# Routed attention with a GELU feed-forward block on one Trainium2 core: where and when the 64-bit weights are rounded

## The chip, the cores and the metric

The kernel runs on one NeuronCore of a Trainium2 chip. The engines named below are TensorE (PE in the profile, with its weight loads as PEld), VectorE (DVE), ScalarE (ACT), GpSimd (POOL) and SyncE (SP, which here only issues DMAs). The metric is the device time of one execution in microseconds (us). The kernel before was timed five times: median 1053.18 us, from 1050.35 to 1054.77 us.

## What is computed

Attention with 4 batches, 8 heads, 768 tokens and head size 64. Every query and every key is assigned to the nearest of 16 centroids of its head, and a query sees only the keys of its own cluster:

```python
q_assign = argmax(q_n @ c_n); k_assign = argmax(k_n @ c_n)      # per head
mask = q_assign[:, :, :, None] == k_assign[:, :, None, :]
scores = where(mask, scale * q @ k.T, -1e9)
x = softmax(scores) @ v            # -> (3072, 512)
h = x @ w_in                       # 512 -> 2048
g = h * 1 / (1 + exp(-1.702 * h))
out = g @ w_out                    # 2048 -> 512
```

q, k, v and the centroids are fp32. The two weight matrices come as 64-bit floats, and the kernel makes fp32 numbers of them on the chip: this is the "rounding" that the change is about.

## The kernel before, in words

**Units and turns.** A pair is two heads of one batch; there are 16 pairs. The scores of a pair are made transposed, in units of 128 keys by 384 queries of both heads; 12 units make a pair, 192 units the whole. Six units that share their queries are a group g (32 groups). The main loop runs over turns t = 0 to 97, with two units each in turns 0 to 95. In a turn TensorE makes the scores (L393) and, in the first batch (turns 0 to 23), adds a one-hot product (L407) that pushes masked scores away; ScalarE takes the exponentials (L418); in the later batches VectorE masks them (L429); GpSimd adds the units of a group up (L439); TensorE multiplies the units of the turn before with v (L450). Two turns after the end of a group `normalise(g)` sums over the keys on TensorE (L462), VectorE takes the reciprocal (L465) and multiplies (L467). `check(g)` lets ScalarE add up the reciprocals and a function of them (L477, L479): these sums decide at the end whether the fast path was safe.

**Preparation.** `prep_*` steps of the next pairs (transposes L271, products with the centroids L285, the assignment L296 to L317, the one-hots L358 or the spread codes L332) are dealt to turns by the table `prep_at`.

**The feed-forward block inside the turns.** When group 3 is normalised (turn 13) the first half of batch 0 goes into the queue `half_ffn`: 16 pieces `first` (L516, four matmuls with `w_in`, then `gelu`) and 12 pieces `second3` (L496, four matmuls with `w_out`). When group 7 is normalised, 48 pieces of the other half follow in `ffn` (L545 and L496). A turn adds a rate to the counter `owed` and takes as many pieces: 28/11.5 = 2.43 a turn from `half_ffn`, 0.62 a turn from `ffn`, the latter until 8 pieces are left. These 8 run after the last turn, before the remaining three batches go through a feed-forward stage of their own (`first7` with L733, `second7` with L790).

**Rounding a weight chunk.** The weights are cut into NW = 32 chunks of 128 x 512 numbers, 16 of `w_in` and then 16 of `w_out`. SyncE loads a chunk as pairs of 32-bit words into one of three `raw` buffers (L155). `split_w` takes the exponent bits (L168) and the mantissa bits (L170) of the high words on VectorE, and turns each into its floating-point part on ScalarE (L172, L174). One call later `join_w` puts the sign to the power (L180), adds the low words (L183) and multiplies (L186), all on VectorE. `round_next()` issues the load of chunk i+2, `split_w(i)` and `join_w(i-1)`. It is called once in turns 1, 2, 4, 5, 6, 8, 9 and 10, and from turn 12 on twice a turn, three times in odd turns, until all is done; `round_to` calls it where a piece needs a chunk that is not there.

**What sets the order.** The program is under a manual schedule: each engine runs its instructions in the order in which the code writes them. So what stands in front of what on an engine is read directly from the loop. Tile pools bound how far engines may drift apart: three PSUM banks `m` (`bank()`) for preparation, normalising and feed-forward pieces, two PSUM score buffers, four `A` buffers, three `raw`, two `e`.

Of the kernel before, what the change touches and what calls it, by code (L numbers as in the profile page):

```python
# [38 lines left out]
def fast(  # L39
# [26 lines left out]
    nc = tc.nc  # L66
# [20 lines left out]
    const = ctx.enter_context(tc.tile_pool(name="const", bufs=1))  # L87
# [15 lines left out]
        name="dram", bufs=2, space=bass.MemoryType.DRAM))  # L103
# [3 lines left out]
    def bank():  # L107
        return ps_m.tile([P, 512], FP32, name="m")
# [17 lines left out]
    def load_v(p):  # L126
# [16 lines left out]
    w_chunks = [  # L143
        (w[:, c, n:n + WN],
         src.bitcast(I32)[c * P:(c + 1) * P, 2 * n:2 * (n + WN)])
        for w, src, n_c, n_n in ((w_in, moe_w_in, NCH, DF),
                                 (w_out, moe_w_out, NF, DM))
        for n in range(0, n_n, WN) for c in range(n_c)]
    NW = len(w_chunks)
    w_raw, w_pow = {}, {}  # L150

    def load_w(i):
        if i < NW:
            t = wp.tile([P, WN, 2], I32, name="raw")
            nc.sync.dma_start(out=t.rearrange("p n t -> p (n t)"),  # L155
                              in_=w_chunks[i][1])
            w_raw[i] = t

    EXP = 0x7FF00000

    def split_w(i):

        hi = w_raw[i][:, :, 1]
        w = w_chunks[i][0]
        e = wp.tile([P, WN], I32, name="e", bufs=2)
        nc.vector.tensor_scalar(out=e, in0=hi, scalar1=EXP, scalar2=None,  # L168
                                op0=ALU.bitwise_and)
        nc.vector.tensor_scalar(out=w.bitcast(I32), in0=hi, scalar1=0xFFFFF,  # L170
                                scalar2=None, op0=ALU.bitwise_and)
        nc.scalar.activation(out=e, in_=e, func=AF.Relu, scale=8.0,  # L172
                             bias=low[:, 0:1])
        nc.scalar.activation(out=w, in_=w.bitcast(I32), func=AF.Copy,  # L174
                             scale=2.0 ** -20, bias=1.0)
        w_pow[i] = e

    def join_w(i):
        raw, e, w = w_raw.pop(i), w_pow.pop(i), w_chunks[i][0]
        nc.vector.scalar_tensor_tensor(  # L180
            out=e, in0=raw[:, :, 1], scalar=-2 ** 31, in1=e,
            op0=ALU.bitwise_and, op1=ALU.bitwise_or)
        nc.vector.scalar_tensor_tensor(  # L183
            out=w, in0=raw.bitcast(U32)[:, :, 0], scalar=2.0 ** -52, in1=w,
            op0=ALU.mult, op1=ALU.add)
        nc.vector.tensor_tensor(out=w, in0=w, in1=e.bitcast(FP32),  # L186
                                op=ALU.mult)

    w_done = [0]

    def round_next():
        i = w_done[0]
        if i < NW:
            load_w(i + 2)
            split_w(i)
        if 0 < i <= NW:
            join_w(i - 1)
        w_done[0] += 1

    def round_to(n):  # L200
        while w_done[0] <= min(n, NW):
            round_next()

    load_qk(1, 0)
# [6 lines left out]
    nc.vector.tensor_copy(out=ident_h, in_=ident)  # L211
    half = const.tile([P, 1], FP32, name="half")
    nc.vector.memset(half, 0.5)
    low = const.tile([P, 1], FP32, name="low")
    nc.vector.memset(low, -896.0 * 2.0 ** 23)
    top = const.tile([P, 1], FP32, name="top")
    nc.vector.memset(top, 2.0 * LIMIT)
    twos = const.tile([P, D], FP32, name="twos")
# [7 lines left out]

    hot = hp1.tile([P, NJ * 4, 32], BF16, name="hot")
    nc.vector.memset(hot, 0.0)
    row_sums = const.tile([P, 2, 2 * NPAIR], FP32, name="sums")

# [9 lines left out]
                            op0=ALU.add)  # L240
# [230 lines left out]
    recs = {}  # L471

    def check(g):


        rec = recs.pop(g)
        nc.scalar.activation(out=rec, in_=rec, func=AF.Copy,  # L477
                             accum_out=row_sums[:, 0, g:g + 1])
        nc.scalar.activation(out=rec, in_=rec, func=AF.Relu, bias=top[:, 0:1],  # L479
                             scale=-2.0 * LIMIT * LIMIT,  # L480
                             accum_out=row_sums[:, 1, g:g + 1])
# [22 lines left out]
    half_ffn, ffn = deque(), deque()  # L504
# [63 lines left out]
    NT = NU // 2  # L568
    TG = NJ // 2
    TB = 2 * HP * TG  # L570

    prep_at = {}
    for p in range(1, NPAIR):
        b, hp = divmod(p, HP)
        for i in range(2 if p == 1 else 0, len(PREP)):
            if p == 1:
                t = (i - 2) // 2
            elif b == 0:
                t = (hp - 2) * TG + 1 + i // 2
            else:  # L580
                t = b * TB + TG * hp - (7, 7, 6, 6, 4, 3, 2)[i]
# [5 lines left out]
    def prep(p, i):  # L587
        if i == 0 and p:
            load_v(p)
        PREP[i](p)  # L590
        if i in (1, 3) and loads:
            load_qk(*loads.popleft())

    rate = (NF + NH * (NF // 4)) / (TB / 2 - 0.5)
    owed = 0.0
    for p, i in [(0, i) for i in range(6)] + [(1, i) for i in range(2)]:
        prep(p, i)
# [2 lines left out]
    for t in range(NT + 2):  # L600
        us = range(2 * t, 2 * t + 2) if t < NT else ()
        for u in us:
            scores(u)
        if t == 0:
            prep(0, 6)
        for u in us:
            part(u)
        for u in us:
            exps(u)
        second_half = t >= TB // 2  # L610
        if second_half:
            round_next()
        if recs:
            check(*recs)
        for u in us:
            mask(u)
        work = sorted(prep_at.get(t, ()), key=lambda w: PREP[w[1]] != prep_near)
        while work and PREP[work[0][1]] == prep_near:
            prep(*work.pop(0))
        if 1 <= t <= NT:  # L620
            for u in range(2 * t - 2, 2 * t):
                values(u)

        todo = half_ffn or (ffn if len(ffn) > NF // 2 else ())
        owed += (rate if half_ffn else 0.62) if todo else -owed
        g = (t - 2) // TG if t >= 2 and (t - 2) % TG == TG - 1 else None
        if g is not None and second_half:
            normalise(g)
        for p, i in work:
            prep(p, i)  # L630
        if g is not None and not second_half:
            normalise(g)
        if recs and t < TB:
            check(*recs)
        if second_half or t and t % 4 != 3:
            round_next()
        while owed >= 1 and todo:
            todo.popleft()()
            owed -= 1
        if second_half and t % 2:  # L640
            round_next()
    check(*recs)
    qcode.clear()
    att.close()
# [181 lines left out]
    for b in range(1, B):  # L826
        for f in range(FB):
            if b == 1:
                sums_z(f)
            first7(b, f, *XT)  # L830
            sums_w((b - 1) * FB + f + 2)
        for n in range(NH):
            sg = sums_g(n)
            if (b, n) == (B - 1, 1):
                ps = bank()
                nc.tensor.transpose(out=ps[0:1, 0:P], in_=ok1, identity=ident)
                nc.vector.tensor_reduce(out=okt, in_=ps[0:1, 0:P], axis=AX.X,
                                        op=ALU.min)
                nc.vector.tensor_scalar(out=bad, in0=okt, scalar1=-1.0,
                                        scalar2=1.0, op0=ALU.mult, op1=ALU.add)  # L840
            if (b, n) == (B - 1, NH - 1):
                is_bad = nc.values_load(bad[0:1, 0:1], min_val=0, max_val=1)
            second7(b, n, sg)
            if n == 1 and b < B - 1:
                XT = sums_x(b + 1)
            if (b, n) == (B - 1, 0):


                ok = const.tile([P, 2, 2 * NPAIR], FP32, name="ok")
                nc.vector.tensor_scalar(out=ok, in0=row_sums, scalar1=LIMIT,  # L850
                                        scalar2=None, op0=ALU.is_le)
                ok1 = const.tile([P, 1], FP32, name="ok1")
                nc.vector.tensor_reduce(out=ok1, in_=ok, axis=AX.XY, op=ALU.min)
# [439 lines left out]
```

## Time and profile before

| what | value |
|---|---|
| median of 5 runs | 1053.18 us |
| the profiled execution, its own time | 1052.68 us |
| its span in the trace | 1050.9 us |
| mean granted TensorE clock | 0.982 |
| PE busy in the span | 998.9 us (95%) |
| DVE busy | 686.3 us (65%) |
| ACT busy | 365.3 us (35%) |
| POOL busy | 389.1 us (37%) |

The span is 1.8 us shorter than the execution's time; that lies around it and is no part of the trace. The profile's page has the busy shares in 40 slices of the span, the chain of work that ended last, and groups of instructions with their count, busy time and mean duration. The trace answers the same for any stretch (a window), for one source line, and as a timeline of single instructions. A line such as "L439 POOL TENSOR_TENSOR sum<-sum,A" says: line 439 of the kernel, on GpSimd, writes tile `sum` from `sum` and `A`.

The turns can be told in the timeline by their scores (L393). Turn 1 starts at 17.2 us of the span, turn 5 at 40.6, turn 9 at 65.1, turn 14 at 89.6, turn 17 at 136.9, turn 20 at 167.5, turn 21 at 187.8, turn 26 at 249.1, turn 32 at 280.1. The last scores (turn 95) start at 584.7, the 8 pieces after the turns at 594.8, and the feed-forward stage at 609.9.

### The profile page before, as it was taken

Reading aid. Unit: us, or ns where it says so; the run is one execution under the profiler, and the core shown is the slowest. Engines: PE = TensorE matmul, PEld = TensorE weight load, DVE = VectorE, ACT = ScalarE, POOL = GpSimd, SP = SyncE. Lnnn points to the kernel's source line nnn. Section 1 sums busy time; section 2 is a strip of 40 time slices with the busy share of each in tenths; the row PEclk is TensorE's granted clock in tenths of the full one; section 3 lists DMA queues with packets and bytes.
Section 4 is the critical chain, followed back from the end, with each engine's and each line's share of the span. In section 5 each row is a group of like instructions: output and inputs, shape, how many; then the busy total and the mean of one; then the engine's idle time right before and its main releaser. Section 6 shows DMA issues by size and latency. Waiting matters only on the chain.

```text
span 1050.9 us, 12464 instructions
## 1 busy us (share of the span) xinstructions
PE 998.9 (95%) x4574; PEld 584.1 (56%) x4574; DVE 686.3 (65%) x1079; ACT 365.3 (35%) x697; POOL 389.1 (37%) x280
## 2 busy tenths in 40 slices
PE   7887798999999999999999899999999999999997
PEld 3333353445544455443544355688755788655886
DVE  3889998415877788776877667743477634576431
ACT  3655465323555555445555322200022200122000
POOL 2554322223666466655567847600022100120000
PEclk9998899999999999999999999999999999999999
DMA  7523354122002320032100000000000000000000
GB/s 198 144 66 106 126 152 138 38 65 63 17 0 61 83 71 8 17 75 61 26 1 1 1 11 0 1 21 21 21 0 1 1 21 21 21 0 1 21 21 23
DMA packets 66117, 45.24 MB, mean 43 GB/s; under 512 B 52096, under 2 KB 60032, under 8 KB 66048
## 3 DMA queue, kind: packets, MB, share of 16 engines
q1 hardware_dynamic: 65904, 44.33, 14.9%
q8 instruction: 38, 0.62, 0.3%
q14 instruction: 31, 0.25, 0.1%
q10 hardware_dynamic: 144, 0.03, 0.0%
HBM read 38.04 MB, written 6.31 MB: 42 GB/s over the span
## 4 chain that ended last, share of the span: by engine, by line
PE 83%; DVE 11%; ACT 2%; issue 1%; POOL 1%; DMA 1%; DVEq 0%; ACTq 0%; POOLq 0%
PE b L790 21%; PE b L733 21%; PE s L393 11%; PE o L450 9%; PE m L496 8%; PE m L545 4%; DVE short L465 2%; PE m L516 2%; PE m L271 2%; DVE A L429 2%; PE m L462 2%; DVE e L168 1%; PE m L285 1%; DVE e L180 1%; DVE w_in L186 1%
## 5 line engine op out<-in xcount | busy, mean ns | idle before, releaser
L439 POOL TENSOR_TENSOR sum<-sum,A 128x768 f32<-128x768 f32 x128 | 235.7, 1841 | 201.4 <-DVE A L429 104.6
L429 DVE SCALAR_TENSOR_TENSOR A<-qb,code,s 128x384 f32<-128x384 uint8 x288 | 157.6, 608 | 94.8 <-ACT s L418 82.1
L393 PE MATMUL s<-T,T 64*128 64x384 f32 x768 | 158.6, 525 | 13.2 <-ACT A L418 9.0
L450 PE MATMUL o<-A,inv 128*64 128x384 f32 x768 | 147.0, 502 | 1.1 <-DVE A L429 1.1
L418 ACT ACTIVATE s<-s 128x768 f32<-128x768 f32 x144 | 109.4, 793 | 83.4 <-PE s L393 72.6
L724 DVE TENSOR_TENSOR G<-b,G 128x384 f32<-128x384 f32 x168 | 93.4, 556 | 51.8 <-PE b L733 45.0
L671 POOL TENSOR_TENSOR W<-w_in 128x256 f32<-128x256 f32 x24 | 17.7, 738 | 263.8 <-PE b L733 262.8
L393 PEld LDWEIGHTS s<-T,T 64*128 64x128 f32 x768 | 66.2, 189 | 86.4 <-issue 23.9
L724 DVE TENSOR_TENSOR y<-b,y 128x256 f32<-128x256 f32 x54 | 22.1, 423 | 130.1 <-PE b L790 93.8
L486 ACT ACTIVATE th<-G 128x384 f32<-128x384 f32 x96 | 50.2, 523 | 159.0 <-DVE G L724 98.4
L733 PE MATMUL b<-x,w_in 128*128 128x384 f32 x288 | 101.2, 486 | 0.0
L450 PEld LDWEIGHTS o<-A,inv 128*64 128x64 f32 x768 | 47.2, 137 | 86.5 <-issue 81.3
L439 POOL TENSOR_TENSOR sum<-A 128x768 f32<-128x768 f32 x32 | 59.5, 1861 | 93.0 <-ACT A L418 43.3
L465 DVE RECIPROCAL short<-m 128x384 f32<-128x384 f32 x32 | 81.7, 2552 | 13.7 <-PE m L462 13.6
L487 DVE SCALAR_TENSOR_TENSOR G<-th,G 128x384 f32<-128x384 f32 x96 | 68.6, 714 | 16.9 <-ACT th L486 14.2
L733 PEld LDWEIGHTS b<-x,w_in 128*128 128x128 f32 x288 | 54.7, 190 | 37.9 <-issue 0.5
L733 PE MATMUL b<-x,W 128*128 128x384 f32 x192 | 69.8, 486 | 0.0
L516 PE MATMUL m<-x,w_in 128*128 128x384 f32 x128 | 51.3, 559 | 15.6 <-ACT short L291 4.9
L790 PE MATMUL b<-Z,G 128*128 128x256 f32 x288 | 65.1, 379 | 0.0
L790 PE MATMUL b<-w_out,G 128*128 128x256 f32 x288 | 63.6, 379 | 0.0
L790 PEld LDWEIGHTS b<-w_out,G 128*128 128x128 f32 x288 | 54.6, 190 | 8.1
L790 PEld LDWEIGHTS b<-Z,G 128*128 128x128 f32 x288 | 54.7, 190 | 7.4
(115 smaller groups left out, 1310.6 us busy)
## 6 DMA issues: line engine op xcount, KB each, us to landing
raw<-in_moe_w_in_dram SPq DMA_DIRECT2D x16, 512.0 KB, 3.9
raw<-in_moe_w_out_dram SPq DMA_DIRECT2D x16, 512.0 KB, 3.7
in<-in_q_dram SPq DMA_DIRECT2D x32, 192.0 KB, 3.0
in<-in_k_dram SPq DMA_DIRECT2D x32, 192.0 KB, 4.0
inv<-in_v_dram SPq DMA_DIRECT2D x16, 384.0 KB, 4.3
out_dram<-y SPq DMA_DIRECT2D x15, 256.0 KB, 2.1
qb<-line SPq DMA_DIRECT2D x12, 192.0 KB, 3.3
out_dram<-y SPq DMA_DIRECT2D x18, 128.0 KB, 1.8
```

What stands on the lines that cost most here:

```text
L393: nc.tensor.matmul(out=ps[:, a, 0:HALF], lhsT=T[p, 1][rows, kt * P:(kt + 1) * P], rhs=T[p, 0][rows, h * HALF:(h + 1) * HALF], start=True, ...
L418: nc.scalar.activation(out=A_of[u] if p < HP else s, in_=s, func=AF.Exp, scale=SCALE)
L429: nc.vector.scalar_tensor_tensor(out=A_of[u][:, a, :], in0=qcode[p][:, a, h * HALF:(h + 1) * HALF], scalar=code[p][:, kt % NH, 1, kt // NH ...
L439: nc.gpsimd.tensor_tensor(out=sum_of[g], in0=A_of[u - 1] if kt == 1 else sum_of[g], in1=A, op=ALU.add)
L450: nc.tensor.matmul(out=o_of[g][a * D:(a + 1) * D, 0:HALF], lhsT=v_in[p][:, a, kt, :], rhs=A[:, a, :], start=(kt == 0), stop=(kt == NJ - 1))
L465: nc.vector.reciprocal(out=rec, in_=ps[:, 0:HALF])
L487: nc.vector.scalar_tensor_tensor(out=g, in0=t, scalar=1.0, in1=h, op0=ALU.add, op1=ALU.mult)
L496: nc.tensor.matmul(out=ps[:, 0:DM], lhsT=g, rhs=w_out[:, f, :], start=(f == 0), stop=(f == NF - 1))
L516: nc.tensor.matmul(out=ps[:, 0:HALF], lhsT=w_in[:, c, f * P:(f + 1) * P], rhs=xT[c], start=(c == 0), stop=(c == NCH - 1))
L724: nc.vector.tensor_tensor(out=o, in0=p, in1=a, op=ALU.add)
L733: nc.tensor.matmul(out=ps[:, 0:HALF], lhsT=a[:, c], rhs=x(c), start=(c == 0), stop=(c == 1))
L790: nc.tensor.matmul(out=ps[:, 0:DN], lhsT=a(f // 4)[:, f % 4], rhs=z(f), start=(f == 0), stop=(f == FB - 1))
```

## The change

`split_w` and `join_w` become one `round_next` of five operations, each of which takes the result of the one before. The bits of the fp32 number are shifted into place (two operations), the power is cut out of it, the low words are scaled by the power, and the two parts are added. ScalarE no longer takes part in the values. Until turn 13 VectorE does the last addition, and from turn 5 on the first four operations use a PSUM bank `m` for the number instead of the weights' own place in SBUF; from turn 14 on GpSimd does the last addition and everything lies in SBUF. `check_w`, one chunk later, lets ScalarE test the range of the high words, with two activations that also add up along the row. The table `pace` deals the calls to turns: one in turns 0, 2, 5, 8, 9, 11, 12, 13, two in every turn from 14 on (one early, one at the turn's end; the one of turn 13 at its end). `half_ffn` is dealt at 1.6 pieces a turn, `ffn` at 0.65; in the last turns (from 93) the queue `ffn` goes down to 4 pieces instead of 8, at 1.0 a turn. `check(g)` stands only behind the exponentials of the next turn, no more directly behind `normalise(g)` in the first batch. The core of the diff:

```diff
-    def split_w(i):
-        hi = w_raw[i][:, :, 1]
-        w = w_chunks[i][0]
+    def round_next(in_psum=False, engine=nc.gpsimd):
+        i = w_done[0]
+        if i - 1 in w_read:
+            check_w(i - 1)
+        if i == NW:
+            return
+        load_w(i + 2)
+        raw, w = w_raw.pop(i), w_chunks[i][0]
         e = wp.tile([P, WN], I32, name="e", bufs=2)
-        nc.vector.tensor_scalar(out=e, in0=hi, scalar1=EXP, scalar2=None,
+        a = bank() if in_psum else w
+        hi, lo, a_i = raw[:, :, 1], raw.bitcast(U32)[:, :, 0], a.bitcast(I32)
+        nc.vector.tensor_scalar(out=a_i, in0=hi, scalar1=3, scalar2=0x3FFFFFF8,
+                                op0=ALU.logical_shift_left,
+                                op1=ALU.bitwise_and)
+        nc.vector.scalar_tensor_tensor(out=a_i, in0=hi, scalar=ODD, in1=a_i,
+                                       op0=ALU.bitwise_and, op1=ALU.bitwise_or)
+        nc.vector.tensor_scalar(out=e, in0=a_i, scalar1=POWER, scalar2=None,
                                 op0=ALU.bitwise_and)
...
+        e = e.bitcast(FP32)
+        nc.vector.scalar_tensor_tensor(out=e, in0=lo, scalar=2.0 ** -52, in1=e,
+                                       op0=ALU.mult, op1=ALU.mult)
+        engine.tensor_tensor(out=w, in0=a, in1=e, op=ALU.add)
+        w_read[i] = raw
         w_done[0] += 1
 
+    def check_w(i):
+        y = w_read.pop(i).bitcast(FP32)[:, :, 1]
+        nc.scalar.activation(out=y, in_=y, func=AF.Square,
+                             accum_out=row_sums[:, 2, i:i + 1])
+        nc.scalar.activation(out=y, in_=y, func=AF.Exp, scale=-2.0 ** 12,
+                             bias=fifteen[:, 0:1],
+                             accum_out=row_sums[:, 3, i:i + 1])
...
-    rate = (NF + NH * (NF // 4)) / (TB / 2 - 0.5)
+    rate = 1.6
+    pace = {t: 1 for t in (0, 2, 5, 8, 9, 11, 12, 13)}
+    pace.update((t, 2) for t in range(TB // 2 + 2, NT))
...
-        if second_half:
-            round_next()
+        how = ((False, nc.gpsimd) if t >= TB // 2 + 2 else
+               (t > 2, nc.vector))
+        if pace.get(t) and t != TB // 2 + 1:
+            round_next(*how)
...
-        todo = half_ffn or (ffn if len(ffn) > NF // 2 else ())
-        owed += (rate if half_ffn else 0.62) if todo else -owed
+        kept = NF // 2 if t < NT - 3 else NF // 4
+        todo = half_ffn or (ffn if len(ffn) > kept else ())
+        owed += (rate if half_ffn else 0.65 if kept > NF // 4 else 1.0) if todo else -owed
...
-        if recs and t < TB:
-            check(*recs)
-        if second_half or t and t % 4 != 3:
-            round_next()
         while owed >= 1 and todo:
             todo.popleft()()
             owed -= 1
-        if second_half and t % 2:
-            round_next()
+        if pace.get(t) == 2 or t == TB // 2 + 1:
+            round_next(*how)
```

The sums that decide on the fast path (`row_sums`, `ok`) have four rows of 32 instead of two.

More of the change, by code (lines that the diff above doesn't have):

```diff
@@ L157, in load_w @@
             w_raw[i] = t
-    EXP = 0x7FF00000
-    def split_w(i):
-        hi = w_raw[i][:, :, 1]
-        w = w_chunks[i][0]
-        e = wp.tile([P, WN], I32, name="e", bufs=2)
-        nc.vector.tensor_scalar(out=e, in0=hi, scalar1=EXP, scalar2=None,
-                                op0=ALU.bitwise_and)
[L170 to L197, printed above, removed]
-        w_done[0] += 1
+    ODD = -2 ** 30
+    POWER = -2 ** 23
+    w_done, w_read = [0], {}
+    def round_next(in_psum=False, engine=nc.gpsimd):
[6 more added lines that the diff above has]
+        raw, w = w_raw.pop(i), w_chunks[i][0]
+        e = wp.tile([P, WN], I32, name="e", bufs=2)
+        a = bank() if in_psum else w
[6 more added lines that the diff above has]
+        nc.vector.tensor_scalar(out=e, in0=a_i, scalar1=POWER, scalar2=None,
+                                op0=ALU.bitwise_and)
+        e = e.bitcast(FP32)
[3 more added lines that the diff above has]
+        w_read[i] = raw
+        w_done[0] += 1
@@ L200, in round_to @@
+    def check_w(i):
[5 more added lines that the diff above has]
+                             accum_out=row_sums[:, 3, i:i + 1])
     def round_to(n):
-        while w_done[0] <= min(n, NW):
+        while w_done[0] < n:
             round_next()
@@ L213, in fast @@
     nc.vector.memset(half, 0.5)
-    low = const.tile([P, 1], FP32, name="low")
-    nc.vector.memset(low, -896.0 * 2.0 ** 23)
+    fifteen = const.tile([P, 1], FP32, name="fifteen")
+    nc.vector.memset(fifteen, 15.0)
     top = const.tile([P, 1], FP32, name="top")
@@ L228, in fast @@
     nc.vector.memset(hot, 0.0)
-    row_sums = const.tile([P, 2, 2 * NPAIR], FP32, name="sums")
+    assert NW == 2 * NPAIR
+    row_sums = const.tile([P, 4, NW], FP32, name="sums")
     csq = short()[:, 0:D]
@@ L846, in fast @@
             if (b, n) == (B - 1, 0):
-                ok = const.tile([P, 2, 2 * NPAIR], FP32, name="ok")
+                ok = const.tile([P, 4, NW], FP32, name="ok")
                 nc.vector.tensor_scalar(out=ok, in0=row_sums, scalar1=LIMIT,
```

## The prediction

> **What bounds the kernel now.** I read the busy shares by slice, then windows cut at the turns, then the waits and the timeline of the bad stretch.
>
> ```profile
> PE   7887798999999999999999899999999999999997
> ...
> DVE  3889998415877788776877667743477634576431
> ...
> PEclk9998899999999999999999999999999999999999
> ```
>
> A slice is 26.3 us. TensorE is nearly full everywhere but in slices 1 to 7 (to 185 us), where VectorE is at 8 to 9 tenths and the granted clock dips, and a little near slice 22. Windows, with columns window, length, busy of PE, PEld, DVE, ACT, POOL, then clock:
>
> ```profile
> 17.20:40.60 23.40, 22.57 (x151) 10.33 (x150) 13.21 (x19) 14.62 (x26) 14.86 (x8) 0.94 0.50 136
> 40.60:65.10 24.50, 18.69 (x117) 7.40 (x115) 22.68 (x30) 13.77 (x27) 10.86 (x6) 0.92 0.37 98
> 65.10:89.60 24.50, 21.27 (x110) 7.72 (x110) 22.95 (x23) 15.37 (x27) 16.26 (x8) 0.87 0.28 86
> 89.60:136.90 47.30, 36.57 (x122) 17.00 (x122) 45.84 (x61) 22.63 (x42) 13.13 (x7) 0.86 0.38 117
> 136.90:167.50 30.60, 30.60 (x135) 15.75 (x134) 28.60 (x42) 17.70 (x34) 10.11 (x5) 1.00 0.51 151
> 167.50:187.80 20.30, 15.39 (x61) 7.33 (x60) 16.26 (x26) 8.98 (x17) 3.68 (x2) 0.92 0.45 143
> 187.80:249.10 61.30, 60.05 (x225) 25.95 (x224) 20.53 (x31) 16.60 (x31) 14.47 (x8) 1.00 0.15 41
> ...
> 560.00:595.00 35.00, 29.51 (x155) 11.68 (x150) 25.77 (x38) 16.55 (x30) 25.84 (x15) 0.98 0.00 1
> ```
>
> From 40.6 to 136.9 us VectorE is busy 91.5 of 96.3 us and TensorE idles 19.8 us. Where TensorE had idled the clock is 0.86 to 0.92, a second loss. From 187.8 on TensorE is 98% busy at full clock, and from 610 to 1045 entirely: nothing that only unloads other engines pays there. So at stake are turns 1 to 25, and the last turns (560 to 595, idle 5.5 us).
>
> Why VectorE is full: by line, in turns 14 to 20 (89.6 to 187.8) L168, L170, L180, L183 and L186 take 15.8 + 15.3 + 17.6 + 14.4 + 15.9 = 79.0 us of its 90.7, for 21 chunks: 3.76 us each. Undisturbed (0.42, 0.42, 0.68, 0.68, 0.69 us) one is 2.9 us. The rest is this (VectorE, then GpSimd):
>
> ```profile
> 65.43 1.92 DVE L168 TENSOR_SCALAR e<-raw 128x512 int32<-128x512 int32 x1
> 67.27 2.04 DVE L170 TENSOR_SCALAR w_in<-raw 128x512 int32<-128x512 int32 x1
> ```
> ```profile
> 65.16 3.85 POOL L439 TENSOR_TENSOR sum<-sum,A 128x768 f32<-128x768 f32 x2 [2.79 <-ACT A L418]
> ```
>
> A 0.42 us operation behind a running GpSimd addition ends only after it; then they alternate. The excess, 21 x 0.86 = 18 us over 14 additions, is 1.3 us for each. But not every form suffers:
>
> ```profile
> L429 DVE SCALAR_TENSOR_TENSOR A<-qb,code,s x288: 598/608/616, 228.7 to 589.8; 128x384 f32<-128x384 uint8 x144
> ```
>
> With one input in SBUF and one in PSUM none of 288 is longer than 0.616 us, beside additions all the time. Second, ScalarE stands behind this full VectorE. Waits of turns 14 to 20:
>
> ```profile
> ACT e L172 <- DVE e L168: 19.5, 13, 2.7
> ACT short L477 <- DVE x L467: 11.7, 3, 4.4
> ```
>
> While it waits there, exponentials, evacuations and tanh behind it are late, and TensorE waits for those.
>
> **The change part by part. (1) Turns 1 to 13** (72.4 us). TensorE's busy time times the clock is 21.2 + 17.2 + 18.5 = 56.9 us, so at most 15.5 us can be won. Before, rounding took 35.3 us of VectorE's 45.6 between 40.6 and 89.6 (by line: 6.4 + 5.0 + 5.5 + 8.7 + 9.8), for 12 to 13 chunks issued before turn 14. The change issues 8, of which six fall into these turns (5, 8, 9, 11, 12, 13), in PSUM. No row shows these forms at 512 elements; L724 (one PSUM input, 384) takes 0.556, L186 0.69 at 512, so I take 0.69 for each of five, 3.5 us a chunk (from below 0.42 + 0.69 + 0.42 + 0.69 + 0.69 = 2.9). Only the fourth (low words and power, both in SBUF) has the form that waits: six times at most 1.3 us. Sum 6 x 3.5 + 5 = 26 us instead of 35. ScalarE loses the waits for L168 (4.6 us) and for L467 (10.3 us in 40.6 to 89.6), since the check stands in the next turn. What is late next is ScalarE: 29.1 us busy of 49, latency between scores and exponentials included, and the three `m` banks, one of which a chunk now holds for some 4 us. I take half of the gap: **7 us**, bounds 2 and 13.
>
> (The Trainium skill, "SBUF — State Buffer", section "Who interferes with whom", says that a VectorE instruction with two SBUF inputs contends with a GpSimd instruction that reads SBUF and that the loser blocks fully, and that one with at most one SBUF input outside the two-port modes does not. The rows agree for both kinds. The rule speaks against the other half of the change: an addition moved to GpSimd holds the pair itself. If every GpSimd operation blocked for its full length, part 2 would come out as in rival B.)
>
> **(2) Turns 14 to 25** (159.5 us). Before: 28 pieces there. A `first` takes 2.58 us (7.74 for three), a `second3` 3.43; a turn's scores, one-hots and values 1.49 + 0.43 + 1.44, a normalise 0.81 every third turn, preparation about 1.0 a turn from 17. TensorE's floor: 16 x 2.58 + 12 x 3.43 + 12 x 3.63 + 9 = 135 us, so 24.5 us were lost. After, at 1.6 a turn, 19.2 pieces run there: 3 turns of 7.8, 7 of 8.8, 2 of 10.1 = 105 us. The other 8.8 pieces, 30 us, move to turns 26 to 31, which TensorE fills anyway; the `ffn` pieces they displace move on to turn 92. TensorE's total is the same. So the stage gains if its twelve turns take under 159.5 - 30 = 129.5 us, 10.8 a turn.
>
> VectorE per turn: two chunks of four operations in SBUF. They now depend on each other, so they do not overlap: 0.42 + 0.69 + 0.42 + 0.69 + gaps = 2.3 us, 4.6 a turn. Gelu 1.6 x 0.55 = 0.9, reciprocal and product (2.55 + 0.6)/3 = 1.05, assignment from turn 17 (2.2/3) 0.75: 6.6 to 7.3. To this comes blocking. GpSimd: 1.67 group additions a turn at 1.81 us, and two weight additions of 512; between L439 (768: 1.81) and L671 (256: 0.73) that is 1.25 each, together 5.5 us a turn. The early one is followed by gelu and reciprocal, which have one SBUF input; the late one meets the next turn's first operation. With 1.2 for that and 0.5 to 1.3 for each group addition: 2 to 3.4 us. VectorE then needs 9.3 to 10.7 us where TensorE needs 8.8. Turn time about 10: 12 x 10 = 120, gain **9 us**; bounds 24 (TensorE alone) and -15 (rival B). A piece waits for VectorE only through its bank, which smooths this.
>
> ScalarE pays two activations with an accumulator read: 0.62 + 0.72 + 2 x 0.19 = 1.7 us instead of 1.34, 12 us over 32 chunks, under TensorE (ScalarE is 49.3 of 98.2 us busy there). Its words lie two apart; VectorE reads the same at full rate, so I count no extra; at double it is 1.3 us a chunk, still covered. The single table load of 1.3 us stays single; were there two per chunk, it would be 82 us of ScalarE, 2.6 a chunk.
>
> SyncE: the load of chunk i+2 now waits for ScalarE's check of i-1 instead of VectorE's join; q, k, v loads queue behind it. A load lands 3.8 us after issue and is needed a turn later (8 us): nothing, at worst 1 us in a few turns.
>
> **(3) The last turns.** The chain of waits ends so:
>
> ```profile
> 589.75 1.81 POOL sum L439
> ...
> 594.89 15.04 PE m L496 x32
> ```
>
> The idle 5.5 us of 560 to 595 lie at 575.9 (1.7), 587.7 (1.1) and 591.3 (2.2, waiting for GpSimd). Four of the eight pieces (1.88 us each) move into turns 93 to 96, and the slower dealing keeps pieces until turn 92. That fills about 4.5 us. But the 15 us also cover the sums for the next stage: VectorE's reach 606.4, while TensorE would be through its first product at 603.7. It then waits 2 to 3 us. Net **2 us**, bounds -2 and 5. `ok` with four rows: 0.2 us operations, hidden.
>
> Sum: 7 + 9 + 2 = 18 us. On the profiled execution (1052.7; span 1050.9 and 1.8 around it) that is 1034.7; the median is 0.5 above it. I say **1034**.
>
> **Rivals. A: everything is covered.** VectorE drops below TensorE's need, the clock stays at 1.00: gains 13, 22 and 4, so 1014. For it: 136.9 to 167.5 shows full TensorE with VectorE at 93%. Against it: the port alternation stays.
>
> **B: GpSimd and VectorE take turns, slower.** In turns 14 to 25 each of the 3.67 GpSimd operations a turn blocks 1.3 us: 7.3 + 4.7 = 12.0 a turn, 144 us against 129.5, +14.5. Late weight additions hold back group additions, `A` buffers and so exponentials: the other gains shrink to 4. Sum +10: 1063. It decides from 10.8 us a turn (11.6 with the other gains).
>
> **C: given back.** Turns of 11 to 11.5 us, early gain 3: within 3 us of before, 1050 to 1056.
>
> **How the numbers follow.** Forecast 1024 to 1045: 0.58. A: 0.15. Between 1045 and 1050: 0.08. C: 0.07. B: 0.12. The measurement can tell about 0.3% (3.2 us): faster 0.81, same 0.07, slower 0.12. The range 1012 to 1052 takes in A and the weak end and leaves out B and the far ends.
>
> **What would show it.** Turn 14 should start near 82 us instead of 89.6, and turn 32 near 255 instead of 280 (16 us won; 4 to 5 displaced `ffn` pieces of 1.9 us come later); L168's waits on ScalarE gone; the first three operations of turns 5 to 13 never above 0.8 us, the fourth up to 2; in turns 14 to 25 operations near 1.5 to 2 us beside the new GpSimd line of about 1.25 us x24; clock above 0.92; the feed-forward stage 435 us as before, with a short wait at its start. I am wrong if turns 14 to 25 exceed 129 us, or if the chain there still runs through VectorE with TensorE idle over 15 us.

## The result and the profile after

The changed kernel takes 1051.68 us (median of 42 runs; the kernel before, in 70 runs beside it and beside the experiments, 1053.8): ratio 0.9976, 95% interval 0.9969 to 0.9984. So it is faster by 0.24%, some 2 us, and not by the 18 that were forecast. The profiled execution took 1052.49 us, with a span of 1050.6 where the kernel before had 1050.9.

First the busy shares by slice of the changed kernel's page:

```profile
PE   7799878889999999999999999999999999999997
...
DVE  4679877763577878777877677743477634576431
...
PEclk9999888999999999999999999999999999999999
```

VectorE has fallen from 8 and 9 tenths to 6 to 8 in slices 2 to 7 (the fourth stays at 9), as it should. TensorE is hardly fuller there, and the clock dips in slices 5 to 7 (105 to 184 us). Emptying VectorE alone has not filled TensorE. Windows of the changed kernel, cut at the starts of turns 1, 5, 17, 20, 22 (columns as before):

```profile
17.30:45.40 28.10, 23.25 (x149) 10.90 (x148) 12.97 (x18) 13.66 (x25) 14.31 (x8) 0.90 0.44 123
...
108.05:141.60 33.55, 28.72 (x117) 13.83 (x116) 29.53 (x37) 20.52 (x48) 18.61 (x13) 0.90 0.47 135
141.60:172.75 31.15, 22.25 (x89) 10.61 (x88) 20.96 (x28) 13.89 (x33) 15.82 (x10) 0.78 0.40 119
```

In turns 20 and 21 (141.6 to 172.75) TensorE is idle for 8.9 of 31.2 us and its granted clock is 0.78, though VectorE is only 67% busy, ScalarE 45% and GpSimd 51%. No engine is full; they wait for each other. Turns 1 to 4 have grown from 23.4 to 28.1 us. The time of each stretch in four profiled executions, and in the forecast (in us, by the starts of the turns; "test late" and "both" are the two mended kernels e9 and f2 below):

| turns | before | changed | test late | both | forecast |
|---|---|---|---|---|---|
| 1 to 4 | 23.4 | 28.1 | 28.3 | 22.1 | with 5 to 13 |
| 5 to 13 | 49.0 | 40.4 | 38.9 | 38.9 | 64.8 for 1 to 13 |
| 14 to 25 | 159.5 | 130.7 | 122.8 | 122.7 | 120 |
| 26 to 31 | 31.0 | 59.8 | 56.7 | 56.8 | 53 |
| start of turn 32 | 280.1 | 276.3 | 264.0 | 257.7 | 255 |
| from there to the end | 770.8 | 774.3 | 772.8 | 773.9 | 778 |

Two executions of the same code differ too: e5 below, which is the kernel before up to turn 25, took 22.0 and 50.9 us in the first two rows, so differences of 2 us in this table say nothing.

The prediction's own bound for turns 14 to 25 was 129.5 us (30 us of pieces move on), and its sign of being wrong was more than 129 us, or TensorE idle over 15 us with the chain through VectorE. The changed kernel takes 130.7 us there, with TensorE idle for 17.9. Turns 14 to 31 together take 190.5 us before and after: nothing was won in them. Of the 8.6 us won in turns 5 to 13, turns 1 to 4 gave 4.7 back, and the time from turn 32 on, where displaced pieces run, another 3.5 (the forecast had 7 there).

What holds turns 14 to 25 is seen in the waits of 85 to 216 us (in total, times, longest):

```profile
ACT raw L197 <- DVE w_in L180: 12.1, 6, 4.4
...
ACT raw L197 <- DVE w_out L180: 6.2, 3, 3.9
...
PE m L520 <- ACT short L295: 6.8, 2, 5.0
```

L197 is the first activation of the range test, and it waits for VectorE. L295 is an evacuation, a copy that empties a PSUM bank so that TensorE can use it again. The chain of waits through one such place (start, duration, what):

```profile
146.76 1.50 DVE w_out L177
148.25 0.02 issue
148.28 0.70 DVE w_out L180
148.98 0.02 issue
149.00 0.77 ACT raw L197 x2
149.77 0.03 issue
149.80 0.85 ACT raw L199 x2
150.65 0.52 ACT short L481 x2
151.17 0.02 issue
151.19 0.71 ACT short L483 x2
151.90 0.37 ACT short L295
```

ScalarE in front of the test, and TensorE behind it, in the timeline (the idle time before the instruction stands in brackets):

```profile
149.00 0.67 ACT L197 ACTIVATE raw<-raw 128x512 f32<-128x512 f32 x1 [3.86 <-DVE w_out L180]
```
```profile
152.31 7.12 PE L520 MATMUL m<-x,w_in 128*128 128x384 f32 x16 [4.96 <-ACT short L295]
```

The test writes its squares over the raw words, so it may not start before L180, the last reader of the high words, has passed. In the order of the program it stands in front of the next `round_next`, that is, ahead of `check(g)` (L481, L483) and of the evacuation L295, which were ready: the product that L295 copies was done at 144.4, and VectorE's last use of the reciprocals of `check(g)` ended at 146.3. ScalarE had been idle for 3.86 us in front of L197 at 149.00. The copy comes only behind the test and the check, and the piece that waits for it on TensorE (L520) at 152.3.

### The profile page after: what moved, and what is told of

It is laid out like the page before. It is cut to its first block, busy times and chain, and to the rows that moved or that the text cites. A ratio compares the mean times of both kernels' runs of the same rounds, so it can differ in the third digit from the quotient of the medians.

```text
span 1050.6 us, 12571 instructions
## 1 busy us (share of the span) xinstructions
PE 999.8 (95%) x4574; PEld 584.6 (56%) x4574; DVE 677.7 (65%) x1055; ACT 374.2 (36%) x761; POOL 419.1 (40%) x304
## 4 chain that ended last, share of the span: by engine, by line
PE 83%; DVE 10%; ACT 4%; issue 1%; DMA 0%; POOL 0%; SPq 0%; DVEq 0%; ACTq 0%; POOLq 0%
PE b L797 21%; PE b L740 21%; PE s L397 11%; PE o L454 10%; PE m L500 7%; PE m L549 4%; PE m L520 3%; PE m L275 2%; PE m L466 2%; DVE short L469 1%; DVE e L185 1%; DVE w_in L180 1%; DVE w_out L180 1%; PE m L289 1%; DVE A L433 1%
## 5 line engine op out<-in xcount | busy, mean ns | idle before, releaser
L397 PE MATMUL s<-T,T 64*128 64x384 f32 x768 | 155.2, 518 | 2.6 <-DVE A L433 0.6
L731 DVE TENSOR_TENSOR y<-b,y 128x256 f32<-128x256 f32 x54 | 22.1, 423 | 130.1 <-PE b L797 93.8
L520 PE MATMUL m<-x,w_in 128*128 128x384 f32 x128 | 52.3, 566 | 11.8 <-ACT short L295 6.8
L500 PE MATMUL m<-w_out,g 128*128 128x512 f32 x120 | 59.8, 617 | 2.3 <-ACT T L280 2.3
```

The lines of the kernel that those rows point to most:

```text
L397: nc.tensor.matmul(out=ps[:, a, 0:HALF], lhsT=T[p, 1][rows, kt * P:(kt + 1) * P], rhs=T[p, 0][rows, h * HALF:(h + 1) * HALF], start=True, ...
L500: nc.tensor.matmul(out=ps[:, 0:DM], lhsT=g, rhs=w_out[:, f, :], start=(f == 0), stop=(f == NF - 1))
L520: nc.tensor.matmul(out=ps[:, 0:HALF], lhsT=w_in[:, c, f * P:(f + 1) * P], rhs=xT[c], start=(c == 0), stop=(c == NCH - 1))
L731: nc.vector.tensor_tensor(out=o, in0=p, in1=a, op=ALU.add)
```

## The experiments

All ratios are to the kernel before, with 95% intervals; the kernel before had a median of 1053.1 to 1053.8 us in each. Unless another kernel is named, an edit is made to the changed kernel (1051.7 us).

**The parts of the change.** e1 lets VectorE do the last addition throughout; e2 keeps the PSUM form, and VectorE's addition with it, from turn 14 on too; e3 has no range test (its rows of the sums are zero); e4 has the old dealing of pieces.

```diff
 e1
-    def round_next(in_psum=False, engine=nc.gpsimd):
+    def round_next(in_psum=False, engine=nc.vector):
...
-        how = ((False, nc.gpsimd) if t >= TB // 2 + 2 else
+        how = ((False, nc.vector) if t >= TB // 2 + 2 else
                (t > 2, nc.vector))
 e2
-    def round_next(in_psum=False, engine=nc.gpsimd):
+    def round_next(in_psum=True, engine=nc.vector):
...
-        how = ((False, nc.gpsimd) if t >= TB // 2 + 2 else
-               (t > 2, nc.vector))
+        how = (t > 2, nc.vector)
 e3
-        if i - 1 in w_read:
-            check_w(i - 1)
...
+    nc.vector.memset(row_sums, 0.0)
 e4
-    rate = 1.6
+    rate = (NF + NH * (NF // 4)) / (TB / 2 - 0.5)
```

> The changed kernel with the last addition on VectorE in all turns (in SBUF from turn 14 on), instead of GpSimd from turn 14. Theory P (the weight addition on GpSimd holds the port and holds up the next operation of the following chunk, L180 at 1.65 instead of 0.69 us): L180 falls back to about 0.7 to 0.9 us on average, L177 to 0.45, which saves some 14 us of VectorE in turns 14 to 25; the addition costs 24 x 0.7 = 17 us there. So about the same time as the changed kernel, within 3 us. Theory S (ScalarE's range test, which waits for VectorE, holds up the copies behind it): the same time too, since VectorE is as late as before. A rival, that GpSimd's free time matters (group additions late): 4 us or more faster.

1058.8 us, 1.0053 [1.0034, 1.0073]: GpSimd's addition is worth 7 us. Neither theory had that, nor the rival.

> The changed kernel with the PSUM form and VectorE's addition also from turn 14 on. Theory P: only the fourth operation (two SBUF inputs) can be held up, by the group additions alone; a chunk takes 5 x 0.7 = 3.5 us of VectorE against 3.2 measured for four operations now, so VectorE is not relieved, and one of three m banks is taken for 3.5 us twice a turn: 3 to 10 us slower than the changed kernel. If the port were the whole of it and the bank cost nothing: 3 to 6 us faster.

1069.6 us, 1.0151 [1.0128, 1.0173]: 18 us more, beyond both expectations. Of these e1 has 7, for e2 also gives VectorE the addition; the PSUM form itself costs some 11. All its operations but the fourth stay at 0.68 to 0.70 us beside GpSimd's sums. But it makes VectorE's chunk longer (0.69 us for each operation, where the undisturbed SBUF form has 0.42 to 0.69), and it holds one of the three `m` banks; the two were not told apart.

> The changed kernel without the range test on ScalarE (check_w is left out, its rows of the sums are set to zero; the values are computed in full). Theory S: ScalarE no longer waits for VectorE's second operation (21 us of waits) and no longer spends 52 us; the copies and exponentials behind it come on time; of the 32 us that TensorE loses in turns 14 to 28, 6 to 10 come back: about 1042 to 1045. Theory P alone: ScalarE is not the bound (45% busy there), so at most 2 us faster.

1035.5 us, 0.9831 [0.981, 0.9852]: 16 us come back, more than either theory gave. What the prediction had put "under TensorE" costs as much as the gain that is missing.

> The changed kernel with half_ffn dealt at 2.43 pieces a turn as before, all else as changed. Theory P and S: at two chunks a turn VectorE needs some 10 us a turn, TensorE with 2.43 pieces 10.5 to 11 instead of 8.8; so TensorE is fuller while the rounding lasts, and more of VectorE's delay is covered: 3 to 8 us faster than the changed kernel. The rival, that the slower dealing of pieces is itself the gain: 3 us or more slower.

1063.2 us, 1.0099 [1.0075, 1.0122]: the slower dealing pays 11.5 us. Both theories had the old rate faster; the rival was right.

**What of the test costs: its work, its wait or its place?** e7 writes the squares into a scratch tile, so that the test only reads the raw words and need not wait for VectorE's reading; e10 tests the chunk that was just issued, which lengthens the wait; e9 puts the test at the end of the turn, behind the pieces.

```diff
 e7
+        seen = yp.tile([P, WN], FP32, name="y")
-        nc.scalar.activation(out=y, in_=y, func=AF.Square,
+        nc.scalar.activation(out=seen, in_=y, func=AF.Square,
...
-        nc.scalar.activation(out=y, in_=y, func=AF.Exp, scale=-2.0 ** 12,
+        nc.scalar.activation(out=seen, in_=seen, func=AF.Exp, scale=-2.0 ** 12,
 e10 (round_next)
-        if i - 1 in w_read:
-            check_w(i - 1)
...
         w_done[0] += 1
+        check_w(i)
 e9 (round_next, and the end of the turn)
-        if i - 1 in w_read:
-            check_w(i - 1)
...
+        for i in sorted(w_read):
+            check_w(i)
         if pace.get(t) == 2 or t == TB // 2 + 1:
             round_next(*how)
```

> The changed kernel, its range test the same two activations, but with results in a scratch tile instead of over the raw words. So the test reads what the DMA brought and waits for nothing of VectorE; ScalarE's work is the same. Theory W (the test's wait for VectorE is what costs): nearly all of what leaving the test out gave comes back, 1036 to 1040 us. Theory L (ScalarE's load of 1.6 us a chunk costs): 1049 to 1052 us. A share of both lies between.

1045.9 us, 0.9926 [0.9908, 0.9944]: without the wait, 6 us less. In the waits of 85 to 212 us the test no longer stands.

> The changed kernel with the test of chunk i directly behind its own round instead of one chunk later: the wait of ScalarE for VectorE is as long as it can be, the work is the same. Theory W: 8 to 20 us slower than the changed kernel, 1060 to 1072 us. Theory L: no change, within 3 us of 1052.

1070.1 us, 1.0159 [1.0137, 1.018]: 18 us more. In the waits of 85 to 230 us of this kernel (its lines are one or two lower) the test's wait has grown, and with it that of TensorE for the evacuation queued behind it:

```profile
ACT raw L196 <- DVE w_out L178: 20.4, 14, 5.5
ACT raw L196 <- DVE w_in L178: 13.9, 7, 5.4
...
PE m L519 <- ACT short L294: 12.2, 2, 7.8
```

> The changed kernel with the tests of a turn's chunks at the turn's end, behind the tanh of the pieces and in front of the late round, instead of in front of each round. Theory W: by then VectorE is through with these words in most turns, so the wait mostly goes, but what is left stands in front of the next turn's exponentials: 1038 to 1046 us. Theory L: the same load, 1050 to 1053 us. The load of the next words waits longer for the test, which could cost some of it again.

1038.5 us, 0.9855 [0.9833, 0.9876]: 13 us less with the same two activations 32 times. Only some 3 us of the 16 that e3 shows are left for the work itself and what waits remain. This is the waits view of the same turns (here 84.5 to 207.3 us, lines two lower) of e9:

```profile
ACT raw L195 <- DVE w_in L178: 3.6, 3, 1.6
...
ACT raw L195 <- DVE w_out L178: 2.3, 3, 1.6
...
PE m L518 <- ACT short L293: 1.9, 2, 1.1
```

The waits have shrunk from 18.3 us (12.1 + 6.2) to 5.9, and TensorE's waits for L293, the old L295, from 6.8 to 1.9. One other path by which the test could cost is that the load of the next words waits for it. It is not the cause: in the changed kernel VectorE's waits up to 230 us name no load of weights (in e9 they do, 2.8 us in all).

**The last turns alone.** e5 is the kernel before with only the change of `kept` and of the dealing of `ffn`; f3 is the changed kernel with 8 pieces left for the end.

```diff
 e5, on the kernel before
-        todo = half_ffn or (ffn if len(ffn) > NF // 2 else ())
-        owed += (rate if half_ffn else 0.62) if todo else -owed
+        kept = NF // 2 if t < NT - 3 else NF // 4
+        todo = half_ffn or (ffn if len(ffn) > kept else ())
+        owed += (rate if half_ffn else 0.65 if kept > NF // 4 else 1.0) if todo else -owed
 f3
-        kept = NF // 2 if t < NT - 3 else NF // 4
+        kept = NF // 2
```

> The kernel before with only the last turns changed (ffn at 0.65, from turn 93 on down to 4 pieces at 1.0 a turn). By the trace of the changed kernel TensorE lost 3.6 us there between 560 and 595 and gave 2 of them back at the start of the next stage: 1.5 to 4 us faster than before. If the pieces were only moved from one covered place to another: no change.

1057.9 us, 1.0049 [1.0031, 1.0066]: on the kernel before it costs 4 to 5 us, against both expectations. Why was not followed up.

> The changed kernel with 8 pieces left for after the turns, as before, all else as changed. By the trace the last turns of the changed kernel lose 0.5 us and the start of the next stage 3.1, together 3.6 against 7.2 before: so 2 to 4 us slower than the changed kernel. On the kernel before, the same edit cost 4.5 us; if it costs here too: 2 to 5 us faster.

1049.6 us, 0.9968 [0.995, 0.9986], against 0.9976 [0.9969, 0.9984] of the changed kernel: no difference that can be told. Windows show why. First the changed kernel, then f3:

```profile
580.00:600.00 20.00, 20.00 (x79) 7.57 (x78) 11.73 (x15) 5.97 (x11) 13.36 (x10) 1.00 0.00 1
600.00:615.00 15.00, 12.45 (x30) 6.06 (x29) 9.64 (x13) 2.39 (x6) 8.10 (x10) 0.89 0.05 17
```
```profile
580.00:600.00 20.00, 17.00 (x72) 6.39 (x71) 12.96 (x16) 7.94 (x16) 16.51 (x15) 1.00 0.00 1
600.00:615.00 15.00, 15.00 (x41) 7.48 (x40) 8.82 (x12) 1.06 (x2) 5.43 (x6) 1.00 0.05 17
```

The changed kernel has filled the 3.0 us that f3 is idle in the last turns. Instead it is idle for 2.5 us at the start of the next stage, whose first product waits for VectorE's sums, and the clock there is 0.89.

**The chunk of turn 2.** The timeline of VectorE in the changed kernel, and TensorE at the end of the gap:

```profile
26.07 0.42 DVE L177 TENSOR_SCALAR w_in<-raw 128x512 int32<-128x512 int32 x1
26.53 2.24 DVE L180 SCALAR_TENSOR_TENSOR w_in<-raw,w_in 128x512 int32<-128x512 int32 x1
28.80 1.91 DVE L182 TENSOR_SCALAR e<-w_in 128x512 int32<-128x512 int32 x1
30.75 0.69 DVE L185 SCALAR_TENSOR_TENSOR e<-raw,e 128x512 f32<-128x512 uint32 x1
31.47 0.69 DVE L187 TENSOR_TENSOR w_in<-w_in,e 128x512 f32<-128x512 f32 x1
32.20 0.56 DVE L367 COPY qb<-m 64x768 bf16<-64x768 bf16 x1
```
```profile
32.81 0.87 PE L275 MATMUL m<-ident,in 128*128 128x128 f32 x3 [4.72 <-DVE qb L367]
```

The chunk stands ahead of the evacuation of the one-hots (L367) on VectorE, and two of its operations take 2.24 and 1.91 us beside GpSimd's sums (26.4 to 30.4 us). Until L367 has emptied the bank, TensorE waits: 4.7 us. In f1 the test is late and in a scratch tile (e9 with e7). f2 is e9 with the chunk of turn 2 at that turn's end; g1 is f2 with the scratch tile, g2 has the late chunk of turn 2 alone.

```diff
-        if pace.get(t) and t != TB // 2 + 1:
+        if pace.get(t) and t not in (2, TB // 2 + 1):
             round_next(*how)
...
-        if pace.get(t) == 2 or t == TB // 2 + 1:
+        if pace.get(t) == 2 or t in (2, TB // 2 + 1):
             round_next(*how)
```

> Both edits of the test at once: results in a scratch tile (no wait for VectorE) and at the turn's end (nothing of the same turn behind it). Measured alone they gave 6 us and 13 us, leaving the test out gave 16. If the wait and the place are separate costs: 1035 to 1037 us, as without the test. If both cure the same wait: as the test at the end alone, 1038 to 1040.

1036.8 us, 0.9851 [0.9825, 0.9877]. The median lies in the range for two separate costs, 1.3 us above e3 and 1.7 below e9; but the ratio cannot be told from that of e9 (0.9855). So a late test pays little or nothing for its wait; g1 below says the same.

> The test at the turn's end, and also the chunk of turn 2 at that turn's end instead of in front of the one-hots' evacuation on VectorE, for which TensorE waited 4.7 us in turn 2. If that wait is on the path: 1033 to 1036 us, turn 3 starting near 29 instead of 33.7. If another wait takes its place (the product of turn 1 and the clock): no change from 1038.5.

1033.4 us, 0.9806 [0.9781, 0.9831]: the best of all, and the forecast of 1034 to within 1 us. Its VectorE in turn 2:

```profile
27.73 0.56 DVE L365 COPY qb<-m 64x768 bf16<-64x768 bf16 x1 [1.16 <-PE m L360]
28.32 0.59 DVE L175 TENSOR_SCALAR w_in<-raw 128x512 int32<-128x512 int32 x1
```

The evacuation comes first, 4.5 us earlier, and turns 1 to 4 are back at 22.1 us.

> Scratch result, test at the turn's end, and the chunk of turn 2 late. If the wait of the test is gone with the place, no better than test at the end and turn 2 late (1033.4 us, within 2). If a separate wait was left: 1029 to 1031.

1033.3 us, 0.9801 [0.9781, 0.9821]: as f2, so beside the late test no cost of the wait is seen.

> The changed kernel with nothing but the chunk of turn 2 moved to that turn's end. If the wait in turn 2 is a cost of its own: 5 us faster than the changed kernel, about 1046.5. If the later losses swallow it: 1050 to 1052.

1041.6 us, 0.9886 [0.9867, 0.9905]: alone it brings 10 us, twice the 5 that it adds to e9. In its profile turns 1 to 4 are 7 us shorter and turns 14 to 25 another 2, which two executions of the same code can differ by; where the rest comes from was not followed up.

**The other parts again, on the mended kernel.** With the two obstacles gone, each remaining part is priced anew. f4 is e9 with VectorE's additions (the edit of e1); g3 is f2 with the old rate (the edit of e4; if a second test is due, the older is done first), h2 with 1.4; g4 is f2 with 8 pieces left; h1 is f2 with `check(g)` directly behind `normalise(g)` in the first batch, as it was before.

```diff
 h1
         if g is not None and not second_half:
             normalise(g)
+        if recs and t < TB:
+            check(*recs)
```

> The test at the turn's end, with the last addition on VectorE in all turns instead of GpSimd. With the test where it was, the same edit cost 7 us. If VectorE's time is the bound of turns 14 to 25, its 24 additions of 0.7 us cost more than the port gives back (L180 back to 0.7 to 0.9 us): 2 to 7 us slower than 1038.5. If the held-up L180 were the bound: 2 to 6 us faster.

1047.1 us, 0.9946 [0.9933, 0.996]: 8.6 us above e9, so GpSimd's addition is worth 7 to 9 us in both. In turns 14 to 25 VectorE's busy time rises by 5.6 us (110.3 to 115.9) and the stage by 10.3 (122.7 to 133.0).

> Test at the turn's end and turn 2 late, with 8 pieces left for after the turns. If the last turns give what the trace showed (idle gone there, part of it back as a wait of the next stage): 1 to 4 us slower than 1033.4. If they give nothing, as on the changed kernel: within 1.5 us.

1033.8 us, 0.9806 [0.9786, 0.9826]: again no difference.

> Test at the turn's end and turn 2 late, with half_ffn dealt at 2.43 again. With the test where the change has it, that cost 11 us. If dealing slowly is needed because VectorE's evacuations of the pieces wait behind the rounding: 5 to 12 us slower than 1033.4. If it only spared ScalarE while the test was in the way: within 3 us.

1056.5 us, 1.0029 [1.0016, 1.0043]: the old rate costs 23 us. TensorE's waits of 78 to 230 us name the reason:

```profile
PE m L500 <- POOL w_out L187: 15.8, 7, 5.0
```

The pieces of the second product catch up with the rounding, and wait for chunks that GpSimd has not yet added. In f2, at 1.6, TensorE's waits have no such line.

> The changed kernel with the tests at the turn's end and the chunk of turn 2 late (1033 us), with the half batch dealt at 1.4 pieces a turn instead of 1.6. Theory that the stage of turns 14 to 25 is still bound by VectorE and GpSimd (some 10 us a turn where TensorE needs 8.8): less work dealt into it means nothing lost there and more left for the full turns after it; 1029 to 1032. Theory that the rest of the loss does not come from the dealing: pieces dealt later displace others only; 1032 to 1035, and above it if the queue is not emptied in time.

1041.9 us, 0.9901 [0.9883, 0.9919], above the ranges of both theories: dealing slower still costs 8.5 us too. Windows of turns 22 to 25, of h2 and then of f2:

```profile
156.50:199.00 42.50, 31.58 (x146) 14.62 (x146) 40.25 (x56) 27.68 (x66) 22.33 (x15) 1.00 0.50 155
```
```profile
157.70:201.00 43.30, 38.99 (x164) 17.65 (x163) 39.80 (x58) 27.65 (x65) 23.34 (x16) 1.00 0.53 165
```

VectorE is 95% busy in h2 and TensorE only 74%. The twelve turns 14 to 25 take 121.2 us instead of 122.7, though TensorE has fewer pieces in them: the turn's length, 10.1 us, is not TensorE's, and the engine that is nearly full is VectorE. Fewer pieces only leave TensorE empty. The pieces not done there come later (turns 32 to 35 take 27.1 us instead of 18.4), where TensorE is full.

> The changed kernel with the tests at the turn's end and the chunk of turn 2 late (1033 us), in which check(g) stands again directly behind normalise(g) in the first batch, as it did in the kernel before. Theory of the prediction (the step that takes ScalarE's waits for L467 away is worth something of its own): ScalarE waits once more for each of 8 groups, 3 to 4 us each in the trace of before, exponentials behind it; 1037 to 1042. Theory against: those waits were late only because VectorE was full; with VectorE emptied, the product is done early and the step costs at most 1 us a group on an engine that has room: 1032 to 1035.

1048.7 us, 0.9961 [0.9947, 0.9974]: 15 us above f2, more than either theory gave. The waits of 17 to 270 us on ScalarE of h1, then the same line of f2:

```profile
ACT short L479 <- DVE x L469: 39.9, 8, 10.1
```
```profile
ACT short L479 <- DVE x L469: 5.2, 5, 1.7
```

At the seven groups whose check is moved ScalarE stands still for 3.2 to 10.1 us each, and turns 14 to 25 take 133.9 us instead of 122.7. VectorE is busy for 76% of them: the step does not need a full VectorE to cost something, which was the theory against it.

## Why the prediction was wrong

**The step that failed** is in part (2): "ScalarE pays two activations with an accumulator read: ... 1.7 us instead of 1.34, 12 us over 32 chunks, under TensorE (ScalarE is 49.3 of 98.2 us busy there)". The duration was right (in the trace 0.68 + 0.19 + 0.77 + 0.19 us, 1.65 from the first start to the last end). The cover was not: an engine that is half busy gives no cover to an instruction which waits, when evacuations and exponentials stand behind it in the same order. The prediction itself named the old waits of L172 and L477 as the second cause of the loss, and then priced the new test as work alone, at nothing. It cost 16 us (e3). Taking the wait away in the old place gives 6 of them (e7), moving the test behind the pieces 13 (e9), both 15 (f1): so wait and place are nearly all of it, and the work itself is 1 to 3 us (f1 and e9 against e3).

**A second step: part (1) counted no cost for the chunk of turn 2.** It looked at the six PSUM chunks of turns 5 to 13 and at L168's and L467's waits, and passed over the early chunk in SBUF of turn 2, behind which the one-hots' evacuation waits. This costs 5 us beside the late test (f2 against e9), 10 alone (g2).

**Part (3), the last turns:** 2 us forecast, none measured (f3 and g4), and a loss of 4 to 5 us on the kernel before (e5). The wait at the start of the next stage, which the prediction put at 2 to 3 us, measured 2.5; the idle time that was filled in the last turns measured 3.0 instead of 4.5 (f3).

What came is closest to rival C, "given back" (1050 to 1056), which had a chance of 0.07: an early gain of 3.8 us instead of 3, and 10.9 us a turn in turns 14 to 25 where C had 11 to 11.5. C gave no cause for such turns. The sum itself is 1034.7 on the profiled execution, or 1035.2 from the median, not 1034; this changes nothing.

**What held.** With the two places mended the kernel takes 1033.4 us. That this meets the forecast of 1034 is partly luck, for the stages miss it both ways: turns 1 to 13 take 61.0 us (forecast 64.8), turns 14 to 25 122.7 (120), turns 26 to 31 56.8 (53), the time from turn 32 on 773.9 (778). The turn time did hold: 10.2 us where about 10 stood. GpSimd's addition takes 1.28 us at the median with `w_out` (1.25 was said). In the tile views of the changed kernel (shortest, median and longest in ns) the operations are as described:

```profile
L180 DVE SCALAR_TENSOR_TENSOR w_in<-raw,w_in x10: 692/1646/2240, 15.1 to 127.3; 128x512 int32<-128x512 int32 x10
L177 DVE TENSOR_SCALAR m<-raw x6: 680/684/687, 48.7 to 89.1; 128x512 int32<-128x512 int32 x6
L180 DVE SCALAR_TENSOR_TENSOR m<-raw,m x6: 695/695/696, 49.4 to 89.8; 128x512 int32<-128x512 int32 x6
```
```profile
L187 POOL TENSOR_TENSOR w_out<-w_out,e x16: 1262/1277/1402, 134.2 to 221.5; 128x512 f32<-128x512 f32 x16
```

With one input in PSUM, 0.68 to 0.70 us every time; with both in SBUF, up to 2.24. The moved `check(g)`, counted only as ScalarE's lost waits, is worth 15 us (h1). Rival B did not come: GpSimd's addition gains 7 to 9 us. The likely reason is that it takes 0.69 us a chunk off VectorE, the engine that is nearly full (h2). In f4 VectorE's busy time accounts for 5.6 us of the 10.3 by which the stage grows; the rest is not accounted for. Here the measurement decides against a reading of the Trainium skill ("SBUF — State Buffer", "Who interferes with whom"): its rule that the port pair which VectorE and GpSimd share is an exclusive lock agrees with the 1.65 us of L180, but it does not say which engine is the scarce one. The same skill ("GPSIMD Engine Reference", "Engine selection") advises to leave elementwise additions to VectorE, since GpSimd takes about twice as long; the rows agree on the durations (1.28 against 0.69 us), and e1 and f4 show that the advice would have cost 7 to 9 us in this kernel.

**What stays open:** why g2 alone brings 10 us, why e5 loses 4 to 5, and most of what still empties TensorE in f2 in turns 17 to 25 (12 of 99.7 us), where VectorE is 88% busy. The longest single wait there, 3.7 us, is one of preparation for a bank that VectorE's reciprocal (L467 in f2) has still to read (waits of 78 to 230 us):

```profile
PE m L273 <- DVE short L467: 4.2, 2, 3.7
```

## What to carry to other kernels

Ask of every instruction that is added to an engine's order, however short, what it waits for and what stands behind it; a busy share of 45% is no cover for a wait. Put such work behind what others wait for, at the end of the turn. And when the parts of a change meet in one stage, run each part again once the obstacle is gone: prices found beside the obstacle (11.5 us for the dealing, 10 for the chunk of turn 2) were 23 and 5 without it.

## What the runs showed of the hardware

- Idle time cost more than itself. From 114 to 126 us of the changed kernel, behind a gap of 3.73 us, the granted clock was 0.72, and the eight matmuls of a piece took 5.02 us instead of 2.85:

```profile
115.68 0.90 PE L275 MATMUL m<-ident,in 128*128 128x128 f32 x3 [3.73 <-DVE short L469]
117.21 5.02 PE L520 MATMUL m<-x,w_in 128*128 128x384 f32 x8 [0.63 <-DVE x L491]
122.71 2.85 PE L520 MATMUL m<-x,w_in 128*128 128x384 f32 x8 [0.48 <-ACT T L280]
```

  PE's busy time was 999.8 us in the changed kernel (mean clock 0.980) and 991.5 in f2 (0.991), with the same 4574 matmuls. The share of idle time alone does not set the clock: turns 20 and 21 of the changed kernel were 29% idle, in gaps of 5.0 and 3.4 us, at 0.78; turns 22 to 25 of h2 were 26% idle, with no gap over 2.2 us but one of 3.9 at their end, at 1.00. No run varied the gaps alone.
- A `TENSOR_SCALAR` with one input in SBUF is not safe from GpSimd either: L182 took 0.43 us alone and up to 1.93 beside a sum, while with its input in PSUM it stayed at 0.69 (shortest, median and longest in ns):

```profile
L182 DVE TENSOR_SCALAR e<-w_in x10: 426/427/1928, 15.8 to 129.6; 128x512 int32<-128x512 int32 x10
L182 DVE TENSOR_SCALAR e<-m x6: 690/691/691, 50.1 to 90.6; 128x512 int32<-128x512 int32 x6
```
